# The two halves of a shared score tile: their order kept by VectorE's queue in place of GpSimd's, and the second half placed ahead of another tile

## The chip, the cores and the metric

The kernel runs on one core of a Trainium2 chip. The core has five engines, each with a queue of its own that it works through in order: TensorE (PE in the profile, and PEld for its weight loads), VectorE (DVE), ScalarE (ACT), GpSimd (POOL) and SyncE (SP, which issues transfers here). They wait for each other by semaphores. TensorE multiplies a stationary operand, loaded as weights, with a moving operand, and writes the product into PSUM, a small memory of eight banks; a bank holds 128 x 512 floats. The metric is the time of one execution on the device in microseconds, as the median of several runs.

## The reference

One block on a sequence of 2048 rows with 512 channels: a layer norm, then an attention with 32 heads of 16 channels and, beside it, a two-layer MLP with 1376 hidden units, whose output gates the attention's.

```python
xn = _layernorm(x, axis=-1)
qkv = (xn @ wqkv).reshape(B, S, 3, H, Dh)          # H = 32, Dh = 16
scores = jnp.einsum("bhqd,bhkd->bhqk", q, k) * (Dh ** -0.5)
p = _softmax(scores, axis=-1)
o = jnp.einsum("bhqk,bhkd->bhqd", p, v)
s = o.reshape(B, S, D) @ wo
g = _silu(gelu(xn @ w1 + b1) @ w2 + b2)
return x + s * g
```

## The kernel before

Operands are split in a high and a low part, so that products of them keep nearly the precision of float32. The attention is cut into 32 units: a unit is a group of four heads with a chunk of 512 queries. Scores are computed twice. The first time, for the row maxima, 128 queries stand as weights and 512 keys move (`s_mm`, L183); VectorE reduces each tile of 128 x 512 scores to maxima of its two halves of 256 keys (`s_max`, L189). There are 2048 such tiles. The second time, transposed and with the maximum taken off, 128 keys stand as weights and the unit's 512 queries move (`t_one`, L732); ScalarE takes the exponential (L734). Then `pv_step` (L797) multiplies the values with the exponentials; it uses all 128 rows of the array and four tiles of 32 columns side by side. When a unit ends, its sums and outputs are copied out of PSUM by ScalarE (L804) and divided later.

Both score products have at most 50 rows, so the array is used as two row tiles: the kernel's `a` is 0 for its upper half of 64 rows and 1 for its lower half. Matmuls of different halves run at the same time. They may not write into one PSUM bank at the same time.

Some 28% of the first scores are made ahead of their use, in the time of the MLP, so the last stage starts with a lead of 576 tiles. From then on a loop over 512 steps runs `t_one` and `pv_step` for one key tile of a unit in each step, and with them so many first scores as the lead asks for: `due(n)` grows by three tiles in a step, until all are made, which gives 490 steps with three. A string of `ORDER` says what such a step issues, one letter after the other:

- T: `t_one`, four in a step, here called T1 to T4. T1 and T2 go to the lower half (`a` 1), T3 and T4 to the upper. After the fourth the step's errands are issued (`todo`: loads, the division, the gate).
- S: `s_whole`, a score tile of 512 keys. The first S of a pair (S1) goes to the upper half, the second (S2), of the same head pair and keys but another head, to the lower.
- X and Y: the third score tile, of which each half of the array makes 256 columns. X makes columns 0 to 255 in the upper half, Y columns 256 to 511 in the lower, for another head; both lie in one PSUM bank. Two steps make the whole of that job. `s_max` follows Y in the code and reduces the bank.
- V: `pv_step` for the key tile of the step before, and the work at a unit's end (transposing the negated maxima by a matmul, L268, and copying them out).

X and Y write one bank from two halves of the array, so Y must wait until X is done. The code makes that wait by hand: after X it puts an empty instruction (`nop`, L221) into a queue of another engine, which waits for X's semaphore and then raises its own, and Y waits for that one. TensorE does not wait otherwise for its own earlier matmul.

The first scores take their banks from a ring of three (`s_ring`). X takes one and holds it until Y's reduction has been issued; a tile's bank comes free when VectorE has reduced it. The second scores have four banks, one for each of a step's T's, which come free by ScalarE's exponentials.

TensorE's weight loads go in the order of the program too, and a wait of a matmul sits on its weight load. VectorE's queue in a step holds the reductions of S1, S2 and the XY tile, and now and then a small instruction: the largest of a unit's maxima (L248), a copy of transposed maxima (L278), a reciprocal (L825). GpSimd's queue holds the empty instructions, the divisions (L834), the splits of the maxima (L251, L252) and the issue of some loads (L109, L112).

Of the kernel before, what the change touches and what calls it, by code (L numbers as in the profile page):

```python
# [36 lines left out]
FILL0 = 38  # L37
HB = 4
W2B = 2
ORDER = {0: "TTTTV", 3: "TXSTTSTYV"}  # L40
HC = CH // 2
PAIRED = 28
KB = 3
# [5 lines left out]
def fused(ctx: ExitStack, tc: tile.TileContext, x, wqk, wv, wo, w1, b1, w2, b2, out):  # L49
    nc = tc.nc  # L50
# [41 lines left out]
    def s_tile(held=False):  # L92
        pool = s_ring.pop(0)
        if not held:
            s_ring.append(pool)
        return pool.tile([P, CH], F32, name="ps"), pool
# [79 lines left out]
    def s_mm(ps, job, a, c0, k0, w):  # L176
        u, st, p = job
        qi, ki = at_of(job)
        if u not in MX:
            MX[u] = qring.tile([P, GH, NCH, NCH, 2], F32, name="mx")  # L180
        r = slice(64 * a, 64 * a + 3 * DH)
        k0 += ki * CH
        return nc.tensor.matmul(ps[:, c0:c0 + w], QS[u][r, p, qi * P:(qi + 1) * P],  # L183
                                kts[u // NCH % KB][p][r, k0:k0 + w], start=True, stop=True).ins

    def s_max(ps, job, heads, parts):
        u, p = job[0], job[2]
        qi, ki = at_of(job)
        nc.vector.tensor_reduce(MX[u][:, 2 * p:2 * p + 2, qi, ki][:, heads, parts], ps.rearrange("p (n c) -> p n c", c=HC), axis=AX.X, op=OP.max)  # L189
        done[u] += 1  # L190
        if ended:
            s_end0(ended.pop())
        if done[u] == 64:
            ended.append(u)
        if done[NU - 1] == 64:
            s_end0(ended.pop())

    def s_whole(job, a):
        ps = s_tile()[0]
        s_mm(ps, job, a, 0, 0, CH)  # L200
        s_max(ps, job, a, slice(0, 2))
# [7 lines left out]
    def s_op(op):  # L209
        if op == "S":  # L210
            if whole:
                s_whole(whole.pop(), 1)
            else:
                whole.append(jobs.pop(0))
                s_whole(whole[0], 0)
        elif op == "X":
            if not cut:
                cut[:] = [jobs.pop(0), 0]
            ps, pool = s_tile(True)
            x = s_mm(ps, cut[0], 0, 0, cut[1] * HC, HC)  # L220
            token = nc.gpsimd.nop().ins  # L221
            tc.add_manual_dep(token, x.name, SYNC, reason="row tile done")
            cut[2:] = [ps, pool, token]
            run_off()
        else:
            job, n, ps, pool, token = cut
            y = s_mm(ps, job, 1, HC, n * HC, HC)
            tc.add_manual_dep(y, token.name, SYNC, reason="other row tile")
            s_max(ps, job, slice(0, 2), n)
            s_ring.append(pool)  # L230
            cut[1] += 1
            if n:
                cut.clear()

    def run_off():
        while put_off:
            put_off.pop(0)()
# [716 lines left out]
    for n in range(L + 1):  # L954
        ua, ka = divmod(n, 16)
        want = due(n) - due(n - 1)
        i = 0
        for op in ORDER[want] if n > 1 else ("TTTTV", "TTTVTSS")[n]:
            if op in "SXY":
                s_op(op)  # L960
            elif op == "V":
                if n:
                    pv_step(*divmod(n - 1, 16))
                for _ in range(4):
                    tick()
                flush()
            else:
                if EARLY <= 4 * n + i < 4 * L:
                    t_one(ua, ka, i % 2, 1 - i // 2)
                for f, args in todo.get((n, i), []):  # L970
                    f(*args)
                i += 1
# [56 lines left out]
```

## Time and profile before

| | |
|---|---|
| median of 3 runs | 1604.39 us (1602.58 to 1605.58) |
| the profiled execution's time | 1603.36 us |
| its span, first to last instruction | 1601.6 us |
| granted TensorE clock over the span | 1.000 |
| steps with three first-score tiles | 490, between 483.2 and 1510.4 us of the span |

The profile gives a time for each instruction. In its rows, the first number of a timeline is the start in us from the span's start, the second the duration; "50*128 50x512" tells a weight tile of 50 rows and 128 columns with 512 moving columns. What stands in brackets is the time that the engine was idle before, and what ended it. In rows of a line or tile, three numbers with slashes are the least, median and largest duration in ns. In rows of groups the numbers behind the bar are busy us, mean ns, and idle us before them. The ends of matmuls are modelled, and one that starts with its weight load shows a longer record. Rows of one kind that follow each other are merged: "x2" at 936.88 is X and S1.

### The profile page before, as it was taken

The page shows a single profiled execution, that of the slowest core. Times are in us where ns is not written, and L with a number is a line of the kernel's source. Part 1 is how long each engine was busy: PE and PEld are TensorE (multiplying, and loading weights), DVE is VectorE, ACT ScalarE, POOL GpSimd, SP SyncE. Part 2 cuts the span into 40 slices and gives each one's busy share as a digit, 9 for nine tenths or more (in the row PEclk, how much of TensorE's full clock was granted, in tenths as well). Part 3 has the DMA queues.
Part 4 walks back from the last instruction along what each step waited for, and adds up shares of the span by engine and source line. Part 5 has one row for each costly group of instructions (what it writes and reads, how often), then busy time and mean ns, then how long its engine had stood idle before and what let it go on. Part 6 is the DMA issues. An engine that isn't in the chain of part 4 may idle for free.

```text
span 1601.6 us, 32363 instructions
## 1 busy us (share of the span) xinstructions
PE 1590.1 (99%) x12132; PEld 914.8 (57%) x12132; DVE 1380.9 (86%) x2257; ACT 1260.4 (79%) x2521; POOL 377.7 (24%) x398
## 2 busy tenths in 40 slices
PE   9999999999999999999999999999999999999998
PEld 7889899999994444444444444444444444444445
DVE  7489898989888999999999989999999999999743
ACT  4333443434349999999999999999999999999984
POOL 4135575756640001000100200100010000000144
PEclk9999999999999999999999999999999999999999
DMA  6625343454331113111410311321141111110252
GB/s 204 149 58 149 118 136 97 152 142 134 113 98 55 40 31 68 29 37 42 80 32 25 69 41 29 60 40 28 31 73 27 31 29 39 32 30 21 62 199 89
DMA packets 76286, 116.92 MB, mean 73 GB/s; under 512 B 24836, under 2 KB 26116, under 8 KB 74952
## 3 DMA queue, kind: packets, MB, share of 16 engines
q1 hardware_dynamic: 72668, 102.42, 22.7%
q0 software_dynamic: 3264, 12.35, 3.9%
q8 instruction: 96, 1.57, 0.4%
q14 instruction: 62, 0.51, 0.1%
q10 hardware_dynamic: 196, 0.07, 0.0%
HBM read 84.35 MB, written 25.97 MB: 69 GB/s over the span
## 4 chain that ended last, share of the span: by engine, by line
PE 97%; DVE 1%; DMA 0%; ACT 0%; issue 0%; SPq 0%; DVEq 0%; ACTq 0%
PE pv L797 32%; PE ps L183 18%; PE pst L732 16%; PE ps L583 12%; PE pst L583 7%; PE ps L732 5%; PE ps L80 3%; PE pv L583 2%; PE pst L80 1%; DVE slot L75 0%; DMA xt<-in_x 0%; DVE st L418 0%; DVE xn L432 0%; DVE slot L893 0%; ACT hh L377 0%
## 5 line engine op out<-in xcount | busy, mean ns | idle before, releaser
L189 DVE TENSOR_REDUCE mx<-ps 128x2 f32<-128x512 f32 x2048 | 1299.1, 685 | 152.9 <-PE ps L183 87.6
L734 ACT ACTIVATE slot<-pst 128x512 f32<-128x512 f32 x1533 | 833.8, 612 | 22.1 <-PE ps L732 8.9
L797 PE MATMUL pv<-slot,vsb 128*32 128x512 f32 x4096 | 545.3, 605 | 0.0
L183 PE MATMUL ps<-kt,slot 48*128 48x512 f32 (+1 forms) x1364 | 393.4, 376 | 0.0
L732 PE MATMUL pst<-qt,kt 50*128 50x512 f32 x1149 | 372.8, 430 | 0.5 <-DVE gt L665 0.4
L732 PEld LDWEIGHTS pst<-qt,kt 50*128 50x128 f32 x1149 | 178.9, 184 | 279.7 <-ACT slot L734 264.0
L734 ACT ACTIVATE slot<-ps 128x512 f32<-128x512 f32 x515 | 315.3, 613 | 4.4 <-PE ps L732 1.2
L183 PEld LDWEIGHTS ps<-kt,slot 48*128 48x128 f32 x1364 | 210.8, 184 | 34.7 <-DVE mx L189 22.1
L583 PE MATMUL ps<-slot,w1h 64*128 64x512 f32 x1088 | 218.5, 393 | 0.4 <-ACT junk L597 0.4
L183 PE MATMUL ps<-kt,qz 48*128 48x512 f32 x512 | 213.0, 416 | 0.0
L183 PE MATMUL ps<-slot,slot 48*128 48x512 f32 (+1 forms) x598 | 172.5, 376 | 0.7 <-DVE mx L189 0.7
L732 PE MATMUL ps<-qt,kt 50*128 50x512 f32 x387 | 162.4, 422 | 0.0
L583 PEld LDWEIGHTS ps<-slot,w1h 64*128 64x128 f32 x1088 | 152.1, 185 | 7.4 <-ACT junk L597 1.7
L797 PEld LDWEIGHTS pv<-slot,vsb 128*32 128x32 f32 x4096 | 80.6, 108 | 120.3 <-issue 112.2
L583 PE MATMUL ps<-slot,w1l 64*128 64x512 f32 x544 | 142.3, 393 | 0.0
L378 POOL TENSOR_TENSOR hl<-hg,hh 128x512 fp32r<-128x512 f32 x76 | 96.8, 1295 | 121.5 <-ACT hh L377 84.7
L597 ACT ACTIVATE junk<-ident_r 1x1 f32<-1x1 f32 x93 | 18.2, 196 | 124.8 <-PE pst L583 120.2
L732 PE MATMUL pst<-qt,slot 50*128 50x512 f32 x384 | 112.6, 416 | 0.0
L251 POOL CAST nmh<-nm 128x16 fp32r<-128x16 f32 x32 | 6.3, 197 | 414.6 <-PE ps L183 111.5
L183 PEld LDWEIGHTS ps<-kt,qz 48*128 48x128 f32 x512 | 93.7, 183 | 16.5 <-issue 0.4
L183 PEld LDWEIGHTS ps<-slot,slot 48*128 48x128 f32 x598 | 92.2, 184 | 17.1 <-DVE mx L189 11.4
L732 PEld LDWEIGHTS ps<-qt,kt 50*128 50x128 f32 x387 | 71.0, 184 | 44.0 <-ACT slot L734 42.8
(150 smaller groups left out, 1711.1 us busy)
## 6 DMA issues: line engine op xcount, KB each, us to landing
raw<-in_w SPq DMA_DIRECT2D x88, 256.0 KB
qk_h<-hh SPq DMA_DIRECT2D x32, 256.0 KB
qk_l<-hl SPq DMA_DIRECT2D x32, 256.0 KB
qt<-qk_h SPq DMA_DIRECT2D x128, 64.0 KB
slot<-qk_h SPq DMA_DIRECT2D x92, 64.0 KB
xt<-in_x SPq DMA_DIRECT2D x16, 256.0 KB
g_d<-gt POOLq DMA_DIRECT2D x16, 256.0 KB, 3.4
qt<-qk_l SPq DMA_DIRECT2D x64, 64.0 KB
```

The source lines that it names most:

```text
L80: nc.tensor.matmul(ps, lhs[a], rhs[b], start=first and n == 0, stop=last and n == 2)
L183: return nc.tensor.matmul(ps[:, c0:c0 + w], QS[u][r, p, qi * P:(qi + 1) * P], kts[u // NCH % KB][p][r, k0:k0 + w], start=True, stop=True).ins
L189: nc.vector.tensor_reduce(MX[u][:, 2 * p:2 * p + 2, qi, ki][:, heads, parts], ps.rearrange("p (n c) -> p n c", c=HC), axis=AX.X, op=OP.max)
L251: nc.gpsimd.tensor_copy(hl[:, 0], nm)
L378: nc.gpsimd.tensor_sub(hl, raw, hh.bitcast(F32))
L583: i = nc.tensor.matmul(ps, lhs[r], rhs[r], start=first, stop=last).ins
L597: i = nc.scalar.activation(junk[:, :1], ident_r[:1, :1].bitcast(F32), AF.Copy).ins
L732: nc.tensor.matmul(ps, kts[g % KB][p][r, k * P:(k + 1) * P], QT[u][r, p, :], start=True, stop=True)
L734: nc.scalar.activation(PT[u, k][:, 2 * p + a, :], ps, AF.Exp, scale=SCALE)
L797: nc.tensor.matmul(PV[u][32 * j:32 * j + 32, :], vsb[:, k, h:h + 32], PT[u, k][:, j, :], start=(k == 0), stop=(k == NT - 1))
```

## The change

Two edits. The string for steps with three tiles has Y ahead of the fourth T and of the second S, where it stood behind both. And the empty instruction between X and Y goes into VectorE's queue instead of GpSimd's.

```diff
-ORDER = {0: "TTTTV", 3: "TXSTTSTYV"}
+ORDER = {0: "TTTTV", 3: "TXSTTYTSV"}
@@ def s_op(op): ... elif op == "X":
             x = s_mm(ps, cut[0], 0, 0, cut[1] * HC, HC)
-            token = nc.gpsimd.nop().ins
+            token = nc.vector.nop().ins
             tc.add_manual_dep(token, x.name, SYNC, reason="row tile done")
```

In the built program TensorE's order in such a step was T1, X, S1, T2, T3, S2, T4, Y, V and is T1, X, S1, T2, T3, Y, T4, S2, V. VectorE's reductions follow: S1, XY, S2 in place of S1, S2, XY; the banks come back to the ring in that order. Errands of a step, which follow T4, stand behind Y and ahead of S2; the small instructions of VectorE and of GpSimd move by one place or two among their neighbours. No matmul, reduction, exponential or transfer is added or taken away.

## The prediction

> **What bounds the kernel now.** I read the page first, then the lines with the empty instruction, then the timeline of two neighbouring steps, engine by engine.
>
> ```profile
> span 1601.6 us, 32363 instructions
> ...
> PE 1590.1 (99%) x12132; PEld 914.8 (57%) x12132; DVE 1380.9 (86%) x2257; ACT 1260.4 (79%) x2521; POOL 377.7 (24%) x398
> ...
> PE 97%; DVE 1%; DMA 0%; ACT 0%; issue 0%; SPq 0%; DVEq 0%; ACTq 0%
> ```
>
> TensorE is nearly always busy and holds the chain of waits, yet a busy TensorE may be one that waits inside a group of row tiles. The groups of the empty instruction and of the waits of weight loads say how often and how long:
>
> ```profile
> L221 POOLq EVENT_SEMAPHORE  x490: 17/17/17, 483.2 to 1510.4; - x164
> ```
> ```profile
> PEld ps L183 <- DVE mx L189: 33.5, 187, 1.0
> ```
>
> There are 490 steps with an X and a Y, from 483.2 to 1510.4 us: 1027.2/489 = 2.101 us a step, 1029.3 us for all 490. In 187 of them a score load waited for VectorE. Two steps in a row, TensorE's matmuls, then the weight loads that matter:
>
> ```profile
> 936.87 0.50 PE L732 MATMUL pst<-qt,kt 50*128 50x512 f32 x1
> 936.88 0.62 PE L183 MATMUL ps<-kt,slot 48*128 48x256 f32 x2
> 937.21 0.52 PE L732 MATMUL pst<-qt,kt 50*128 50x512 f32 x2
> 937.45 0.39 PE L183 MATMUL ps<-kt,slot 48*128 48x512 f32 x1
> 937.57 0.39 PE L732 MATMUL ps<-qt,kt 50*128 50x512 f32 x1
> 937.68 0.28 PE L183 MATMUL ps<-kt,slot 48*128 48x256 f32 x1
> 937.89 1.07 PE L797 MATMUL pv<-slot,vsb 128*32 128x512 f32 x8
> 938.89 0.50 PE L732 MATMUL pst<-qt,kt 50*128 50x512 f32 x1
> ...
> 939.48 0.50 PE L183 MATMUL ps<-kt,slot 48*128 48x512 f32 x1
> 939.58 0.45 PE L732 MATMUL ps<-qt,kt 50*128 50x512 f32 x1
> 939.82 0.28 PE L183 MATMUL ps<-kt,slot 48*128 48x256 f32 x1
> 940.02 1.06 PE L797 MATMUL pv<-slot,vsb 128*32 128x512 f32 x8
> 941.02 0.49 PE L732 MATMUL pst<-qt,kt 50*128 50x512 f32 x1
> ```
> ```profile
> 937.51 0.18 PEld L183 LDWEIGHTS ps<-kt,slot 48*128 48x128 f32 x1
> ...
> 939.48 0.18 PEld L183 LDWEIGHTS ps<-kt,slot 48*128 48x128 f32 x1 [0.17 <-DVE mx L189]
> 939.52 0.18 PEld L732 LDWEIGHTS ps<-qt,kt 50*128 50x128 f32 x1
> ```
>
> Row by row these are T1; X and S1; T2 and T3; S2; T4; Y; V; the next T1. The lower half of the array does T2 at 937.21, S2 at 937.45, Y at 937.68: 0.47 us for two tiles of 512 columns, 0.235 each, so a half tile takes 0.12. V starts 0.21 after Y (937.68 to 937.89), or 0.09 after the half's last column, and holds the array 1.00 us (937.89 to 938.89). This step took 2.02 us with nothing late. In the next, S2's load waited for VectorE until 939.48, 0.59 after T1; Y came at 939.82, 0.34 after that load, so 0.34 - 0.235 = 0.105 passes from a load to its first column, and the step took 2.13. The pair averages 2.075; the mean of 2.101 holds also steps that a copy or another small instruction disturbs. What lets S2 go is the reduction of the step before's Y, third in VectorE's queue:
>
> ```profile
> 937.53 0.69 DVE L189 TENSOR_REDUCE mx<-ps 128x2 f32<-128x512 f32 x1 [0.33 <-PE ps L183]
> ...
> 938.74 0.68 DVE L189 TENSOR_REDUCE mx<-ps 128x2 f32<-128x512 f32 x1
> ```
>
> It ends at 939.42, and the load goes 0.06 later. So a loop of VectorE's third reduction, S2, Y, V and the next S1 sets the time, over two steps.
>
> **The change, part by part.** The lower half's order becomes T1, T2, Y, S2. The loop above goes: S2 now needs only its own bank's reduction, and it stands a quarter microsecond later. What is late next is Y, which may not start until X, in the other half and the same bank, has reported. Before, S2 stood in the time that this report takes; Y's load above went at 937.51, 0.64 after T1, while S2 was streaming. After, nothing of the lower half stands between T2 and Y, and T4's and S2's loads queue behind Y's load; V and all of the next step wait behind S2.
>
> The report takes as long as before, unless the engine matters. GpSimd's event takes 17 ns; VectorE's own wait instructions are these:
>
> ```profile
> L825 DVEq EVENT_SEMAPHORE  x32: 21/21/50, 531.1 to 1470.6; - x32
> L825 DVE RECIPROCAL dr<-dr x32: 240/243/253, 532.5 to 1581.5; 128x16 f32<-128x16 f32 x32
> ```
> ```profile
> L248 DVE TENSOR_REDUCE nm<-mx x32: 274/276/287, 109.8 to 1512.1; 128x16 f32<-128x128 f32 x32
> ```
>
> The two rows of small instructions are needed below. For the event I take 21 ns: 4 ns more, 2 us over 490 steps. The upper bound is 50 ns, 0.033 a step, 16 us. For the lower bound: T1's record ends at 936.87 + 0.50 = 937.37, Y's load follows 0.14 later. A crossing from TensorE to VectorE costs 0.03 (S1's record ends 936.88 + 0.62 = 937.50, its reduction starts 937.53), one back 0.06. If X reported together with T1 and the event cost nothing, 0.09 would be left: Y's load 0.05 earlier, at 0.59. That floor takes X to report no sooner than T1, although its record is shorter:
>
> ```profile
> 936.88 0.39 PE L183 MATMUL ps<-kt,slot 48*128 48x256 f32 x1
> ```
>
> The Trainium skill, "TensorE: Matmul & The Clock Gate", Part 3 (Packing small matmuls), says that matmuls of different tiles start and also end in program order, and that the increments of their semaphores follow one another some 26 ns apart. By that rule X, which stands behind T1, cannot report before 937.37, whatever engine listens, and the sum below holds; by the modelled end of X's record alone (937.27) the first rival below holds. Agreement is indirect here: a 0.14 between T1's end and Y's load leaves 0.05 beside the two crossings.
>
> The new step, then: Y's load at 0.64 + 0.004; first column 0.105 later; Y 0.12; S2 0.235 behind it in the same half (its load has the 0.12 of Y's stream to hide 0.105 in); 0.09 to V; V and its drain 1.00. The sum is 2.19 with rounding, 2.185 with 0.1175 for the half and 0.0875 ahead of V. The upper half is not longer: T4's load goes behind Y's at 0.65 at the soonest, 0.105 + 0.235 makes 0.99, where S2 ends at 1.10.
>
> This must be compared with 2.101, not with 2.075, because the slower step covers what disturbs the faster. VectorE's three reductions end at 939.42, 2.55 after T1; the next step's first comes at 2.185 + 0.66 = 2.845, so 0.30 is free, more than a reciprocal's 0.24 or the 0.28 of L248. ScalarE:
>
> ```profile
> 937.41 1.57 ACT L734 ACTIVATE slot<-pst 128x512 f32<-128x512 f32 x3
> 938.86 0.62 ACT L734 ACTIVATE slot<-ps 128x512 f32<-128x512 f32 x1
> 939.42 1.57 ACT L734 ACTIVATE slot<-pst 128x512 f32<-128x512 f32 x3
> ```
> ```profile
> L804 ACT ACTIVATE os<-pv 128x512 f32<-128x512 f32 x30 | 18.8, 628 | 0.0
> ```
>
> Exponentials follow each other (938.86 - 937.41)/3 = 0.48 apart, so ScalarE is free again at 939.34, 2.47 after T1, and its next is due at 2.185 + 0.54 = 2.725: 0.25 free. One of the 30 output copies, a slot of 0.48 likewise, delays the exponentials by 0.23; T4's tile is then freed at 939.48 - 936.87 + 0.23 - 2.185 = 0.65, and T4's load goes by 0.71, still ahead of S2's first column at 0.86. So the copies cost nothing after; were that cover gone, 30 times 0.23 would add 7 us. Not covered are the transposes of the maxima, which stand ahead of T1 and now push the report too:
>
> ```profile
> L268 PE MATMUL pst<-ident_r,nmh 128*64 128x128 f32 (+1 forms) x9 | 2.4, 267 | 0.0
> L268 PE MATMUL ps<-ident_r,nmh 128*64 128x128 f32 (+1 forms) x4 | 1.1, 268 | 0.0
> ```
>
> These are 13 at 0.27 at most, 3 us. GpSimd loses 490 events of 17 ns and gains nothing that anyone waits for. The DMA issues and errands that stand behind T4 now come ahead of S2 instead of behind both scores, on other queues, and none of them is a wait of TensorE's in these steps.
>
> The sum: 490 x 2.185 + 3 = 1074 us, against 1029: 44 to 45 us more. The profiled execution took 1603.4 us (span 1601.6), 1.0 under the median of 1604.4; with 1.8 around the span as before, the forecast is 1601.6 + 1.8 + 44.6 = 1648 us.
>
> **Rivals.** (A) X reports at its own record's end, ahead of T1, and GpSimd is what is slow: then a report to VectorE lets Y load at 0.40 + 0.03 + 0.06 + 0.02 = 0.51, Y's columns start at 0.615, S2 ends at 0.97, V starts at 1.06, the step is 2.06 and all of VectorE's loop is gone: 490 x (2.06 - 2.101) = -20, 1583 us. It decides where Y's load comes before 0.64 - (2.185 - 2.101) = 0.556. For it: X's record ends 0.11 before T1's. Against it: the floor above, and that the crossings to VectorE and to ScalarE (T1's record ends 937.37, its exponential starts 937.41) fit GpSimd's path with T1 as the start. (B) The floor: load at 0.59 to 0.60, step 2.14, 490 x 0.04 + 3 = 23, 1626 us. (C) VectorE's queue makes the report later, as its empty instruction stands behind the third reduction. That reduction ends at 2.55 - 2.185 = 0.365, ahead of T1's end, so it is free in a plain step; behind a reciprocal or an L248 it is 0.61 to 0.64, some 0.1 late, in the at most 64 steps that have one, 6 us, 1654; with 50 ns an event, 1664. (D) The change does nothing: V's start would have to hang on the upper half alone. T4 at 937.57 ends as late as V allows (937.89 - 0.32), so the upper half permits 2.02, and no row makes it 2.10: 1603 us.
>
> **How the numbers follow.** Forecast 0.70, A 0.05, B 0.10, C 0.13, D 0.02. The range takes in B and C to its 50 ns, and leaves out A and D: 1624 to 1664. Under 0.2%, some 3 us, a measurement of this kernel can't tell from none: faster 0.05 (A), within 0.02 (D), slower 0.93.
>
> **What would show it.** The empty instruction's row should read DVEq, 490 times, some 2.19 us apart, nearly every step alike. Y's load should stand 0.64 after T1 with a wait put down to that row, Y's record should grow by the 0.1 of its load, V should start 1.18 to 1.19 after T1. Score loads should no longer wait for VectorE's reductions, and VectorE should idle some 0.3 in each step. TensorE will still read 99%. I am wrong in the mechanism if Y's load stands before 0.56, or if V's start hangs on T4; wrong in size alone if the load stands at 0.59 or 0.7.

## The result, and the profile after

| | before | after |
|---|---|---|
| median of five runs | 1603.60 us | 1649.38 us |
| range | 1602.55 to 1605.58 | 1649.01 to 1650.30 |
| ratio | | 1.0286, 95% interval 1.0273 to 1.0299 |
| span of the profiled execution | 1601.6 us | 1647.5 us |

The changed kernel is 2.9% slower; the forecast was 1648 us. From the page of the profile after: its span and busy times, the chain, and the group of score weight loads:

```profile
span 1647.5 us, 32368 instructions
...
PE 1635.9 (99%) x12132; PEld 902.5 (55%) x12132; DVE 1380.0 (84%) x2257; ACT 1268.8 (77%) x2521; POOL 377.8 (23%) x398
...
PE 98%; DVE 1%; DMA 0%; ACT 0%; issue 0%; SPq 0%; DVEq 0%; ACTq 0%
...
L183 PEld LDWEIGHTS ps<-kt,slot 48*128 48x128 f32 x1364 | 201.5, 184 | 77.5 <-DVEq L221 77.5
```

The counts are those of before, and so nearly are the busy times of VectorE, ScalarE and GpSimd. TensorE shows 45.8 us more "busy" at the same number of matmuls: the records of the two halves overlap without a gap in the steps below, and one that starts with its weight load is longer, so a wait in one half hides in busy time. The chain says only that TensorE was last. What names the new wait is the last row, and the two views that I had read before, the empty instruction's line and the waits of weight loads in the last stage:

```profile
L221 DVEq EVENT_SEMAPHORE  x490: 21/21/21, 482.9 to 1556.2; - x164
```
```profile
PEld ps L183 <- DVEq L221: 111.4, 487, 0.4
...
PEld ps L183 <- DVE mx L189: 1.2, 2, 1.0
```

The 490 steps now take (1556.2 - 482.9)/489 = 2.195 us where they took 2.101, so the stage has grown by 490 x 0.094 = 46 us: all of the difference. Score loads wait for the empty instruction in 487 of 490 steps; waits for a reduction, 187 before, are down to 2. The timeline of one step, TensorE's matmuls and then its weight loads from T1's to V's:

```profile
943.95 0.50 PE L732 MATMUL pst<-qt,kt 50*128 50x512 f32 x1
943.95 0.61 PE L183 MATMUL ps<-kt,slot 48*128 48x256 f32 x2
944.29 0.51 PE L732 MATMUL pst<-qt,kt 50*128 50x512 f32 x2
944.59 0.38 PE L183 MATMUL ps<-kt,slot 48*128 48x256 f32 x1
944.63 0.45 PE L732 MATMUL ps<-qt,kt 50*128 50x512 f32 x1
944.82 0.39 PE L183 MATMUL ps<-kt,slot 48*128 48x512 f32 x1
945.13 1.06 PE L797 MATMUL pv<-slot,vsb 128*32 128x512 f32 x8
946.13 0.50 PE L732 MATMUL pst<-qt,kt 50*128 50x512 f32 x1
```
```profile
944.17 0.18 PEld L732 LDWEIGHTS pst<-qt,kt 50*128 50x128 f32 x1
944.59 0.18 PEld L183 LDWEIGHTS ps<-kt,slot 48*128 48x128 f32 x1 [0.23 <-DVEq L221]
944.59 0.18 PEld L732 LDWEIGHTS ps<-qt,kt 50*128 50x128 f32 x1
944.70 0.19 PEld L183 LDWEIGHTS ps<-kt,slot 48*128 48x128 f32 x1
```

T1, X with S1, T2 with T3, Y, T4, S2, V, and the next T1. Y's load stands at 944.59, 0.64 after T1, released by the empty instruction; T4's goes at once behind it and S2's when Y streams. V starts 1.18 after T1, the step takes 2.18. VectorE in the same step:

```profile
944.63 1.89 DVE L189 TENSOR_REDUCE mx<-ps 128x2 f32<-128x512 f32 x3 [0.30 <-PE ps L183]
```

Its three reductions leave it 0.30 us idle for TensorE, where before they set the pace of every second step.

### The profile page after: what moved, and what is told of

Its sections match the earlier page's. It is cut to its first block, busy times and chain, and to the rows that moved or that the text cites. A ratio compares the mean times of both kernels' runs of the same rounds, so it can differ in the third digit from the quotient of the medians.

```text
span 1647.5 us, 32368 instructions
## 1 busy us (share of the span) xinstructions
PE 1635.9 (99%) x12132; PEld 902.5 (55%) x12132; DVE 1380.0 (84%) x2257; ACT 1268.8 (77%) x2521; POOL 377.8 (23%) x398
## 4 chain that ended last, share of the span: by engine, by line
PE 98%; DVE 1%; DMA 0%; ACT 0%; issue 0%; SPq 0%; DVEq 0%; ACTq 0%
PE pv L797 31%; PE ps L183 20%; PE pst L732 16%; PE ps L583 12%; PE pst L583 7%; PE ps L732 5%; PE ps L80 3%; PE pv L583 2%; PE pst L80 1%; DVE slot L75 0%; DMA xt<-in_x 0%; DVE st L418 0%; DVE xn L432 0%; DVE slot L893 0%; ACT hh L377 0%
## 5 line engine op out<-in xcount | busy, mean ns | idle before, releaser
L183 PE MATMUL ps<-kt,slot 48*128 48x256 f32 (+1 forms) x1364 | 419.3, 387 | 0.0
L732 PE MATMUL pst<-qt,kt 50*128 50x512 f32 x1149 | 377.6, 435 | 0.5 <-DVE gt L665 0.4
L183 PEld LDWEIGHTS ps<-kt,slot 48*128 48x128 f32 x1364 | 201.5, 184 | 77.5 <-DVEq L221 77.5
L183 PE MATMUL ps<-slot,slot 48*128 48x256 f32 (+1 forms) x598 | 184.5, 388 | 0.7 <-DVE mx L189 0.7
L732 PE MATMUL ps<-qt,kt 50*128 50x512 f32 x387 | 166.0, 431 | 0.0
L183 PEld LDWEIGHTS ps<-slot,slot 48*128 48x128 f32 x598 | 88.6, 184 | 35.5 <-DVEq L221 33.9
```

Source lines behind the costliest of these rows:

```text
L732: nc.tensor.matmul(ps, kts[g % KB][p][r, k * P:(k + 1) * P], QT[u][r, p, :], start=True, stop=True)
```

## The experiments

All times are medians of runs beside the kernel before on the same chip: 1602.9 us for the first four, 1603.1 us for the last four, where the result above had 1603.6. Where a text below says "over all steps", it is the median over the 490 steps of the run's trace, read to the nanosecond.

**The order alone.** The empty instruction goes back to GpSimd.

```diff
-            token = nc.vector.nop().ins
+            token = nc.gpsimd.nop().ins
```

> The new order alone, the empty instruction back in GpSimd's queue. Theory (Y's load waits for X's report, which T1 holds back; the engine that relays it is worth 4 ns a step): within 3 us of the changed kernel, 1645 to 1650 us, step 2.18, Y's load 0.64 after T1. Rival (VectorE's queue is what is slow): most of the 46 us goes away, 1604 to 1615 us. Rival (GpSimd is slower to answer than VectorE): over 1655 us.

1645.7 us (1644.8 to 1646.4), ratio 1.0265 (1.0251 to 1.0280). The loads' waits, and the load that waits in one step whose T1 starts at 943.78:

```profile
PEld ps L183 <- POOLq L221: 107.5, 486, 0.6
```
```profile
944.41 0.18 PEld L183 LDWEIGHTS ps<-kt,slot 48*128 48x128 f32 x1 [0.22 <-POOLq L221]
```

The wait is the same, with GpSimd's name on it, 0.63 after T1. So the order makes nearly all of the loss. VectorE's relay is slower than GpSimd's by 1649.4 - 1645.7 = 3.7 us, or 7.5 ns a step; set against the kernel before of each set it is 45.8 - 42.8 = 3.0 us, 6 ns, and the intervals of the two ratios overlap. The traces settle it: over all steps Y's load stands 0.644 after T1 with VectorE's relay and 0.636 with GpSimd's. The event starts 3 ns later behind the end of T1's record and takes 4 ns more, so 7 to 8 ns a step, nearly twice the 4 ns that the prediction had for it.

**The engine alone.** VectorE's queue, with the old order.

```diff
-            token = nc.gpsimd.nop().ins
+            token = nc.vector.nop().ins
```

> The empty instruction in VectorE's queue alone, the order as before. Theory: Y's columns start when S2 has streamed, 0.81 after T1 at the soonest, while the report lets them start by 0.75, so the relay's engine is hidden: 1602 to 1606 us, no change. Rival (an empty instruction in VectorE's queue delays its reductions or is delayed by them): the loop through the third reduction lengthens by what the instruction costs there, 490 x 0.02 to 0.05 = 10 to 25 us, 1614 to 1630 us.

1608.5 us (1608.4 to 1609.0), ratio 1.0035 (1.0022 to 1.0047): neither of the two, a small loss of 5.6 us. The score loads' waits, then S1 with X and S1's reduction in one step:

```profile
PEld ps L183 <- DVE mx L189: 41.1, 205, 1.0
```
```profile
938.69 0.62 PE L183 MATMUL ps<-kt,slot 48*128 48x256 f32 x2
```
```profile
939.36 3.90 DVE L189 TENSOR_REDUCE mx<-ps 128x2 f32<-128x512 f32 x6 [0.34 <-PE ps L183]
```

No load waits for the empty instruction, so the relay is hidden, as the theory has it. But S1's record ends at 938.69 + 0.62 = 939.31 and its reduction starts 0.05 later; before it was 0.03 (937.50 to 937.53). Over all steps in which VectorE was idle for S1 the two are 0.062 and 0.038. The empty instruction stands ahead of that reduction in VectorE's queue, and the reduction starts some 0.024 later for it, although the instruction ends 0.025 before S1's record does. That loop closes every second step, so 0.024 makes 0.012 a step, 5.9 us over 490. The rival's mechanism is there at the small end of its size. The changed kernel has the same 0.063, but there it costs nothing, since VectorE has time to spare; with the old order it costs, where reductions set the pace.

**X ahead of T1**, in the changed kernel.

```diff
-ORDER = {0: "TTTTV", 3: "TXSTTYTSV"}
+ORDER = {0: "TTTTV", 3: "XTSTTYTSV"}
```

> The changed kernel with X issued ahead of T1 instead of behind it. Theory (matmuls report in program order, so T1's 512 columns hold back the report of X's 256): X reports 0.12 to 0.15 earlier, Y's load goes at about 0.50 after the step's first matmul, Y's columns at 0.60, S2 ends at 0.955, V starts at 1.04, step 2.04 to 2.06; 490 x (2.05 - 2.187) = -67 us against the changed kernel: 1575 to 1592 us, under the kernel before. Rival (the report's time is the relay's and not T1's): Y's load stays 0.62 to 0.65 after the first matmul, 1640 to 1652 us.

1593.3 us (1592.6 to 1594.3), ratio 0.9939 (0.9927 to 0.9952): 56 us under the changed kernel and 0.6% under the kernel before, 1 us beyond the range expected. X, T1 and V of a step and the next X, then the loads of Y, T4 and S2:

```profile
936.31 0.38 PE L183 MATMUL ps<-kt,slot 48*128 48x256 f32 x1
936.31 0.50 PE L732 MATMUL pst<-qt,kt 50*128 50x512 f32 x1
...
937.36 1.06 PE L797 MATMUL pv<-slot,vsb 128*32 128x512 f32 x8
938.35 0.39 PE L183 MATMUL ps<-kt,slot 48*128 48x256 f32 x1
```
```profile
936.80 0.18 PEld L183 LDWEIGHTS ps<-kt,slot 48*128 48x128 f32 x1
936.92 0.18 PEld L732 LDWEIGHTS ps<-qt,kt 50*128 50x128 f32 x1
936.92 0.18 PEld L183 LDWEIGHTS ps<-kt,slot 48*128 48x128 f32 x1
```

X's record ends where it did, 0.38 after it starts. But Y's load now goes 0.49 after X instead of 0.64 after T1. No bracket stands behind it, as the idle time before it is short, yet over all steps it goes 0.050 after the empty instruction's end, as in the changed kernel. A swap of two neighbours that run at the same time in different halves brought the report 0.15 sooner, with the same relay: it was T1 that held it. That leaves a rival. In the trace all of these matmuls count up one semaphore, so whoever waits for X waits for T1's count as well, even if X's came first. ScalarE decides it in the changed kernel's step above, whose T1 starts at 943.95:

```profile
943.74 0.62 ACT L734 ACTIVATE slot<-ps 128x512 f32<-128x512 f32 x1
944.48 1.57 ACT L734 ACTIVATE slot<-pst 128x512 f32<-128x512 f32 x3
```

ScalarE was idle from 944.36 and waited for T1's count, one less than X's. Had X's count come first, at the end of X's record (943.95 + 0.38 = 944.33) or soon after, ScalarE would have gone then. It went at 944.48, after T1's record had ended (943.95 + 0.50 = 944.45). The same holds in all 294 steps of the trace in which ScalarE was idle early enough to tell. So X's completion itself did not come ahead of T1's.

A plain step takes 938.35 - 936.31 = 2.04, as worked out. All steps, though, average more:

```profile
L221 DVEq EVENT_SEMAPHORE  x490: 21/21/21, 482.4 to 1499.8; - x164
```

1017.4/489 = 2.081: 0.04 over the plain step, some 20 us, of which the expectation had at most 10. One such step, with X at 915.34 and the next at 917.73 (2.39), T4's load:

```profile
916.31 0.18 PEld L732 LDWEIGHTS ps<-qt,kt 50*128 50x128 f32 x1 [0.28 <-ACT slot L734]
```

It waits for ScalarE, which ran an output copy ahead of its exponentials (913.67, 0.63 us):

```profile
913.67 0.63 ACT L804 ACTIVATE os<-pv 128x512 f32<-128x512 f32 x1
```

In the trace 26 steps at such copies are about 0.35 longer than the median step and 32 are 0.07 longer, 11 us together. The changed kernel's slow steps cover the copies, which cost 0.1 us in all there; this one is too fast for that. The 13 steps with a transpose of the maxima make 4 us more. The rest, some 4 us, lies in the first of these steps and in scattered ones whose cause stays open.

**X ahead of T1 in the kernel before**, with GpSimd.

```diff
-ORDER = {0: "TTTTV", 3: "TXSTTSTYV"}
+ORDER = {0: "TTTTV", 3: "XTSTTSTYV"}
```

> The kernel before with X issued ahead of T1, GpSimd's queue and the old place of Y kept. Theory (before, the step is set by VectorE's third reduction, which lets S2 go, and the report is hidden behind S2): an earlier report gains nothing, 1600 to 1607 us, steps still alternate between about 2.02 and 2.13, S2's load still waits for VectorE. Rival (the report also set the time before): 1575 to 1595 us.

1602.1 us (1601.3 to 1603.7), ratio 0.9995 (0.9986 to 1.0004): no change. X of one step and of the next, the next one's S2, the X after that, and the load of that S2:

```profile
936.25 0.39 PE L183 MATMUL ps<-kt,slot 48*128 48x256 f32 x1
...
938.26 0.39 PE L183 MATMUL ps<-kt,slot 48*128 48x256 f32 x1
...
938.85 0.49 PE L183 MATMUL ps<-kt,slot 48*128 48x512 f32 x1
...
940.38 0.39 PE L183 MATMUL ps<-kt,slot 48*128 48x256 f32 x1
```
```profile
938.85 0.18 PEld L183 LDWEIGHTS ps<-kt,slot 48*128 48x128 f32 x1 [0.17 <-DVE mx L189]
```

2.01, then 2.12 with S2's load held by a reduction: the alternation of before, untouched. The swap that gains 56 us in the new order gains nothing in the old, though over all steps it brings the empty instruction forward by 0.15 here too. So the report was off the path before and is on it after.

**The report relayed twice**, in the new order.

```diff
             token = nc.vector.nop().ins
             tc.add_manual_dep(token, x.name, SYNC, reason="row tile done")
+            again, token = token, nc.gpsimd.nop().ins
+            tc.add_manual_dep(token, again.name, SYNC, reason="row tile done")
```

> The changed kernel with the report relayed twice: VectorE's empty instruction, then one in GpSimd's queue, then Y. Theory (the report is on the path of every step): a second relay costs what the first shows, 0.024 until it starts, 0.017 for its event, 0.008 until it is seen, 0.05 a step; 490 x 0.05 = 24 us: 1668 to 1678 us, step 2.235. Rival (the step is set by the order of the matmuls or by T4, and the report is not what ends last): 1645 to 1653 us.

1674.2 us (1673.9 to 1675.1): 24.8 more than the changed kernel's 1649.4, 0.051 a step. Y's load in a step whose T1 starts at 943.75, and the first relay's times:

```profile
944.45 0.18 PEld L183 LDWEIGHTS ps<-kt,slot 48*128 48x128 f32 x1 [0.28 <-POOLq L223]
```
```profile
L221 DVEq EVENT_SEMAPHORE  x490: 21/21/21, 483.6 to 1581.1; - x164
```

The load stands 0.70 after T1, and the step takes 1097.5/489 = 2.244, 0.05 more than the 2.195 after: what the report loses, the step loses. No run shows the 0.024 and 0.008 that the expectation added up; in the trace the second event starts 0.033 after the first one's end and takes 0.017, and the load follows it by 0.05 as it followed the first. The sum of 0.05 comes out all the same.

**The report relayed twice in the old order**, the same edit on the run with the engine alone.

> The same second relay with the order of before, to be set against the run with the engine alone changed (1608.5 us). Theory (there the report is hidden behind S2's columns, by a hair: Y's load goes to 0.69, its columns could start at 0.80, where S2 ends at 0.80 to 0.81): 1606 to 1612 us. Rival (the relay costs its time wherever it stands): 1630 to 1636 us.

1610.7 us (1610.5 to 1612.9), 2.2 over the 1608.5 without it. The second relay, 25 us in the new order, is all but hidden here, and score loads wait for reductions as they did with one relay (205 times there):

```profile
PEld ps L183 <- DVE mx L189: 42.3, 208, 1.0
```

**X ahead of T1, Y in its new place, GpSimd's relay.** The order of the third kernel above, with the empty instruction of before.

> X ahead of T1, Y in its new place, and the empty instruction in GpSimd's queue: of the change only the order is kept. Theory (with the report early, T4's load sets the step by waiting for ScalarE's exponential of the step before, a loop of two steps with 2.04 a step; the relay has some 0.1 to spare): 1590 to 1595 us, step 2.04 like the run with VectorE's relay (1593.3 us). Rival (VectorE's 20 ns of relay ahead of its reductions also hold this order back): 5 to 10 us less, 1583 to 1588 us.

1592.1 us (1591.8 to 1594.9), ratio 0.9931 (0.9918 to 0.9945): as the theory has it, within 1.2 us of VectorE's relay. With X early neither the relay nor the delay in VectorE's queue can be seen. The delay is in fact gone: over all steps the reduction starts 0.038 after S1's record in the third kernel too, where the empty instruction ends 0.17 ahead of that. With GpSimd on both sides, the swap of X and T1 is worth 1645.7 - 1592.1 = 53.6 us.

**S2 ahead of T4 as well.**

```diff
-ORDER = {0: "TTTTV", 3: "XTSTTYTSV"}
+ORDER = {0: "TTTTV", 3: "XTSTTYSTV"}
```

> As the last, with S2 ahead of T4, so that S2's load does not queue behind T4's, which waits for ScalarE. Theory (T4 and S2 end together, and V needs both): within 3 us of it. Rival (S2's load behind T4's is what sets V): 5 us or more less.

1590.8 us (1590.4 to 1592.1), ratio 0.9926 (0.9913 to 0.9938). It is the fastest kernel here, 0.7% under the kernel before. Its 1.2 us on the last one are within the spread of both, so whether S2's place beside T4 matters stays open.

## Why the prediction was right

*What bound the kernel before.* The loop through VectorE's third reduction, S2, Y and V was the bound: the change removes that wait (187 to 2), an earlier report alone does nothing (1602.1 us), and 0.024 put into the loop ahead of its reductions costs what a loop over two steps would make of it (1608.5 us).

*What is late next.* Y, for X's report. Y's load stood 0.64 after T1, its record grew from 0.28 to 0.38, V started at 1.18, as foretold. By the rows T4 did not set V: its record ended at 944.63 + 0.45 = 945.08, S2's at 944.82 + 0.39 = 945.21, and S2's ended last in all 490 steps. No run moved T4 alone in this order.

*The relay's engine.* Here a term was mis-sized, within its bounds: 7 to 8 ns a step instead of 4, since of the relay only the event's own 17 and 21 ns had been compared, not when it starts. The changed kernel alone would not have shown it; the run with the order alone did. What the sum did not hold at all is that the empty instruction delays the next reduction by 0.024. In the new order the cover of 0.30 takes it, so the forecast did not suffer.

*The sum.* A step of 2.185 was forecast, 2.191 with the transposes, and 2.195 was measured, 2 us more over 490 steps. The 2.185 has a slip: the 0.004 of the relay is listed and not added. With it the terms make 2.189. Moreover 0.21 from Y to V less 0.1175 leaves 0.0925 ahead of V, not 0.0875, which makes 2.194. Over all steps Y's load stands at 0.644, as the terms say, and V and its drain take 0.996 instead of 1.00, so that the median step is 2.186. The path and the terms were right to a few nanoseconds each; that the total came within 2 us is in part luck, since the slips and the terms taken too large cancel.

*What disturbs the steps.* The faster alternation of before had a mean 0.026 over its pair. After, the median step of 2.186 and the mean of 2.195 lie closer together, 4.2 us over 490 steps, as the slower step covers the copies: they add 0.1 us. The 13 steps with a transpose add 2.6 us, where the prediction had 3, and most of the rest lies in the first of the 490.

*The rivals.* (A), that X reports by its own record, fell: with nothing but X moved ahead of T1 Y's load came 0.15 sooner. The Trainium skill, "TensorE: Matmul & The Clock Gate", Part 3, has matmuls of different tiles end in program order, and this agrees: over all steps the empty instruction starts 0.076 after the end of T1's record when X stands behind T1, and 0.042 after the end of X's own when X stands ahead. By these modelled ends, standing behind T1's report adds 0.034, where the prediction quoted 26 ns between two. (B), the floor, is out by Y's load at 0.64. (C), a report held up behind VectorE's work, is out by the trace: in all but 2 of the 490 steps the empty instruction started 0.565 to 0.580 after T1, and its event took 21 ns in every one. One of the two stood behind a reciprocal, 0.17 late: what (C) describes happened once. (D) is out by the result.

## What to carry to other kernels

Where two pieces of work must not overlap, the cost of their handshake is what stands between them in the queue that waits: here another tile, S2, in the second piece's own half of the array had covered it, and moving the second piece forward to free another wait laid it bare. Before such a move, read how soon the first piece can report, and give it the place ahead of longer work that reports in order; that swap was worth 56 us here, and the choice of the engine that relays 3 to 6 where it mattered, nothing where the report came early. And compare a new steady step with the old mean, not the old best: a slower step also hides what disturbed the faster one.

## What the runs showed of the hardware

A matmul's completion reached the other engines in program order across two row tiles: a half-width one reported 0.15 us later for standing behind a full one that ran beside it, though its own record ended 0.11 sooner. An empty instruction of GpSimd that only passes a semaphore on, put behind the first, added 0.051 us a step. In VectorE's queue, where it ended 0.025 us before the matmul that the reduction behind it waited for, it also made that reduction start 0.024 us later; where it ended 0.17 us before, it did not.
